# Turning the attention output by VectorE block transposes and a DRAM round trip instead of by TensorE, with key sums and row copies moved between engines

## The chip, the cores and the metric

The kernel runs on one core of one Trainium2 chip. The metric is the device time of one execution in microseconds (us), a median over repeated executions. Where a few per cent or less matter, both kernels were timed in rounds on the same chip.

## The reference

Hash attention over q, k, v of shape (4, 8, 768, 64) is followed by an MLP mixer with a token and a channel stage:

```python
q_bits = (np.einsum('bhsd,dk->bhsk', q, proj) > 0)          # 6 hash bits, k alike
mask = q_bucket[:, :, :, None] == k_bucket[:, :, None, :]
scores = np.where(mask, scale * np.matmul(q, k.transpose(0, 1, 3, 2)), -1000000000.0)
...                                                          # softmax over keys, times v
x = attn_out.transpose(0, 2, 1, 3).reshape(B, S, H * D)      # (4, 768, 512)
xt = x.transpose(0, 2, 1)
h = np.maximum(xt @ w_tok1, 0.0) @ w_tok2                    # token stage
u = x + h.transpose(0, 2, 1)
h2 = np.maximum(u @ w_ch1, 0.0) @ w_ch2                      # channel stage
return (u + h2).astype(np.float32)
```

## The kernel before

Attention runs over 16 pairs of heads, four pairs to a batch, and each pair in two halves of 384 queries. It leaves its output in `XT`, with channels on the partitions. The first token product sums over positions, so it needs positions on the partitions. `turn` makes that layout `x` from `XT` with TensorE transposes and ScalarE copies.

```python
def turn(b, x, bank):
    for r in range(0, NR, 2):
        ps = bank()
        for k in range(2):
            at = S * b + P * (r + k)
            for cb in range(NCB):
                nc.tensor.transpose(ps[:, k, P * cb : P * cb + P], XT[:, cb, at : at + P], ident)
        nc.scalar.copy(x[:, r : r + 2], ps)
```

`turn` for batch 0 stands near the end of attention. For batches 1 to 3 it stands in the token stage:

```python
def mix1(b):                                   # first token product
    x = (x0, x1)[b % 2]
    if b:
        turn(b, x, banks)
    ...                                        # 12 matmuls (24 rows of the trace), W1 against x, then Relu to r1
        job()                                  # one weight conversion for the channel stage
def mix2(b):                                   # second token product
    ...                                        # 16 matmuls (32 rows of the trace)
        nc.vector.tensor_tensor(u, ps[:, :HALF], u, op=ALU.add)      # u is a part of XT
        if cb % 2:
            job()
for b in range(B):
    mix1(b)
    if b:
        mix2(b - 1)
...
mix2(B - 1)
```

Weights come as 64-bit numbers. A conversion of 768 columns takes one ScalarE instruction and two on VectorE (`begin`), one more on VectorE with two on GpSimd (`join`), and a Square on ScalarE with a last VectorE instruction (`end`). During attention one third of a conversion is done in each half.

For each pair the exponentials are added up over the six key blocks of a half, partly on GpSimd:

```python
self.a = ...;  nc.gpsimd.tensor_tensor(self.a, es[0], es[1], op=ALU.add)
nc.vector.tensor_tensor(self.d, es[2], es[3], op=ALU.add)
nc.vector.tensor_tensor(self.d, self.d, es[4], op=ALU.add)
...                                            # then es[5], then self.a
```

TensorE sums these over the partitions (`sums`). VectorE refines the reciprocal, copies its rows to their neighbours (`nc.vector.tensor_copy(rec[other...], rec[at...])`), and multiplies (`divide`) into `XT`.

## Time and profile before

The kernel takes 862.65 us (median of 3, 862.43 to 862.66). TensorE's work divides the profiled execution (span 860.9 us) into stages. The first end is read from the chain that ended last, which has a start some 0.07 us later than the timeline's row.

| stage | ends with | at us | length |
|---|---|---|---|
| start | first scores of the first pair's second half | 16.86 | 16.86 |
| attention | first token product | 327.41 | 310.55 |
| token | first channel product | 423.20 | 95.79 |
| channel | VectorE's last addition | 856.9 | 433.7 |
| end | last store landed | 860.9 | 4.0 |

A row of a timeline gives the start, the length, the engine, the line of the program, the operation with its operands and shapes, and the number of instructions in the row. If the engine was idle before it, the length of that and what released it stand in brackets. A row of the view of waits gives the engine, its tile and line, what it waited for, and then the total, the number of times and the longest. The two kernels' line numbers differ. L567, L580 and L586 of before (first token product, second token product, VectorE's update of `XT`) are L598, L617 and L623 of the changed kernel.

Eight token products of about 10.35 us from start to start are 82.8 us of the token stage. The rest of its 95.79 us is transposes (10.4) and a wait of 2.5 us. A matmul of fp32 numbers is two rows of the trace, a transpose one; counts of matmuls below are counts of such rows.

### The profile page before, as it was taken

What the parts mean: (1) busy time and instruction counts of PE and PEld (TensorE: products, weight loads), DVE (VectorE), ACT (ScalarE), POOL (GpSimd) and SP (SyncE); (2) the same over time, 40 slices, a digit from 0 to 9 for tenths busy, and PEclk for the clock granted to TensorE, in tenths of its full rate; (3) what the DMA queues carried; (4) which work ended last, traced back from release to release, by engine and by line L of the source; (5) the groups of instructions that cost most, each with busy time, mean ns of one, the idle gap of its engine ahead of it and who ended that gap; (6) DMA issues with size and microseconds to landing.
All of it is one profiled execution on the core that took longest, in us unless ns stands there. A gap on an engine that the chain in (4) does not pass through costs nothing.

```text
span 860.9 us, 9280 instructions
## 1 busy us (share of the span) xinstructions
PE 847.9 (98%) x3545; PEld 395.2 (46%) x3545; DVE 558.2 (65%) x641; ACT 304.7 (35%) x445; POOL 214.2 (25%) x123
## 2 busy tenths in 40 slices
PE   8999999999999999998999999999999999999997
PEld 4444444444444454554544444444444444444444
DVE  3789999899899895899744483534457332336411
ACT  4666777667776673243012201012110101121000
POOL 3234244424524443166011111101101200011110
PEclk9999999999999999999999999999999999999999
DMA  4334232322332302132102201222210120000001
GB/s 150 106 115 155 112 113 77 112 113 76 115 130 89 130 28 79 68 111 72 38 0 74 73 0 62 86 98 73 73 37 18 43 97 12 1 0 1 24 25 53
DMA packets 20644, 61.16 MB, mean 71 GB/s; under 512 B 2800, under 2 KB 4464, under 8 KB 20592
## 3 DMA queue, kind: packets, MB, share of 16 engines
q1 hardware_dynamic: 20536, 60.46, 19.9%
q8 instruction: 30, 0.49, 0.2%
q14 instruction: 22, 0.18, 0.1%
q10 hardware_dynamic: 56, 0.02, 0.0%
HBM read 53.49 MB, written 6.29 MB: 69 GB/s over the span
## 4 chain that ended last, share of the span: by engine, by line
PE 91%; DVE 5%; DMA 1%; ACT 1%; issue 1%; SPq 0%; DVEq 0%; ACTq 0%
PE b L636 50%; PE sc L299 18%; PE acc L345 14%; PE t L580 3%; PE t L567 3%; PE hp L266 1%; PE sums L369 1%; DVE tmp L170 1%; DVE WC L196 1%; DVE tmp L167 1%; DMA raw<-in_moe_w_ch 1%; DMA qk<-in_qk 0%; DVE esd L334 0%; PE trp L226 0%; DVE T L537 0%
## 5 line engine op out<-in xcount | busy, mean ns | idle before, releaser
L306 ACT ACTIVATE e<-sc 128x768 f32<-128x768 f32 x192 | 151.6, 811 | 26.2 <-PE sc L299 25.6
L299 PE MATMUL sc<-qk 64*128 64x384 f32 x768 | 159.5, 495 | 0.7 <-ACT e L306 0.7
L643 ACT COPY p<-b 128x512 f32<-128x512 f32 x72 | 42.1, 585 | 304.6 <-PE b L636 304.6
L345 PE MATMUL acc<-e,vn 128*64 128x384 f32 x768 | 130.9, 490 | 0.0
L636 PE MATMUL b<-r,WC 128*128 128x512 f32 (+1 forms) x300 | 125.6, 575 | 0.0
L329 POOL TENSOR_TENSOR esa<-e 128x768 f32<-128x768 f32 x32 | 73.0, 2282 | 117.8 <-ACT e L306 101.9
L636 PE MATMUL b<-T,SW 128*128 128x512 f32 x216 | 96.6, 592 | 0.0
L299 PEld LDWEIGHTS sc<-qk 64*128 64x128 f32 x768 | 67.2, 188 | 56.9 <-issue 46.9
L636 PEld LDWEIGHTS b<-r,WC 128*128 128x128 f32 x300 | 57.0, 190 | 67.1 <-issue 64.1
L345 PEld LDWEIGHTS acc<-e,vn 128*64 128x64 f32 x768 | 52.3, 137 | 74.9 <-issue 73.0
L662 POOL TENSOR_TENSOR p<-p,p 128x512 f32<-128x512 f32 x18 | 22.7, 1262 | 249.4 <-ACT p L643 249.4
L185 POOL TENSOR_TENSOR tmp<-tmp,raw 128x768 f32<-128x768 f32 x20 | 43.7, 2183 | 124.8 <-DVE tmp L182 79.1
L666 DVE TENSOR_TENSOR r<-p,u 128x512 f32<-128x512 f32 x18 | 12.5, 693 | 91.4 <-ACT u L643 91.4
L636 PE MATMUL b<-T,WC 128*128 128x512 f32 x144 | 67.7, 592 | 0.0
L636 PEld LDWEIGHTS b<-T,SW 128*128 128x128 f32 x216 | 41.0, 190 | 51.7 <-issue 51.7
L636 PE MATMUL b<-XT,WC 128*128 128x512 f32 x144 | 64.7, 592 | 0.0
L299 PE MATMUL sc<-bits 64*128 64x384 bf16 x384 | 63.2, 323 | 0.7 <-DMA bits<-g 0.7
L636 PE MATMUL b<-r,SW 128*128 128x512 f32 x144 | 62.8, 592 | 0.0
L331 DVE TENSOR_TENSOR esd<-e 128x768 f32<-128x768 f32 x32 | 40.8, 1275 | 19.9 <-ACT e L306 19.9
L332 DVE TENSOR_TENSOR esd<-esd,e 128x768 f32<-128x768 f32 x32 | 45.1, 1408 | 3.3
L351 ACT ACTIVATE num<-acc,vsum 128x384 f32<-128x384 f32 x32 | 18.6, 580 | 80.3 <-PE acc L345 80.3
L186 POOL TENSOR_TENSOR tmp<-tmp 128x768 f32<-128x768 f32 x20 | 45.1, 2257 | 1.6
(84 smaller groups left out, 947.6 us busy)
## 6 DMA issues: line engine op xcount, KB each, us to landing
raw<-in_moe_w_ch SPq DMA_DIRECT2D x16, 768.0 KB
seen<-in_qk SPq DMA_DIRECT2D x16, 768.0 KB
qk<-in_qk SPq DMA_DIRECT2D x15, 768.0 KB
vn<-in_v SPq DMA_DIRECT2D x16, 384.0 KB
vt<-in_vT SPq DMA_DIRECT2D x16, 384.0 KB
out<-p SPq DMA_DIRECT2D x18, 256.0 KB
raw<-in_moe_w_tok SPq DMA_DIRECT2D x4, 768.0 KB
bits<-g SPq DMA_DIRECT2D x124, 5.2 KB
```

The lines of the kernel that those rows point to most:

```text
L185: nc.gpsimd.tensor_tensor(unit, unit, lo, op=ALU.mult)
L186: nc.gpsimd.tensor_tensor(big, big, unit, op=ALU.add)
L299: nc.tensor.matmul(sc[:, i, :HALF], t[rows, 1, P * c : P * c + P], t[rows, 0, qs], start=start, stop=not start,)
L306: nc.scalar.activation(e, sc[:, :, :HALF], ACT.Exp, scale=SCALE)
L329: nc.gpsimd.tensor_tensor(self.a, es[0], es[1], op=ALU.add)
L331: nc.vector.tensor_tensor(self.d, es[2], es[3], op=ALU.add)
L332: nc.vector.tensor_tensor(self.d, self.d, es[4], op=ALU.add)
L345: nc.tensor.matmul(acc[D * i : D * i + D], vn[:, i, c], e[:, i], start=(c == 0), stop=(c == NR - 1),)
L567: nc.tensor.matmul(ps, W1[:, r, P * j : P * j + P], x[:, r], start=(r == 0), stop=(r == NR - 1),)
L580: nc.tensor.matmul(ps[:, :HALF], r1[:, j, P * cb : P * cb + P], W2[:, j, HALF * half : HALF * half + HALF], start=(j == 0), stop=(j == NJ ...
L636: nc.tensor.matmul(self.ps[i][:, cols], left(k), right(k)[:, cols], start=first and k == ks[0], stop=k == ks[-1], skip_group_check=True,)
L643: nc.scalar.copy(c, self.ps[i])
```

## The change

The intent is to take the transposes off TensorE, the bound engine. VectorE turns 32x32 blocks, each where it stands. DMA writes the blocks of two pairs to DRAM in pieces of 256 B and reads a batch back in rows of 2 KB. To make room, GpSimd's additions and conversion steps go to VectorE without GpSimd beside them, ScalarE's first conversion step is folded into one of these, and ScalarE takes the reciprocal's row copies and the mask's product.

```diff
-    nc.sync.dma_start(out=projblk, in_=proj_pair)
+    nc.scalar.dma_start(out=projblk, in_=proj_pair)
 ...                                            # conversion
-            nc.gpsimd.tensor_tensor(unit, unit, lo, op=ALU.mult)
-            nc.gpsimd.tensor_tensor(big, big, unit, op=ALU.add)
+            nc.vector.scalar_tensor_tensor(unit, lo, 2.0**-52, unit, op0=ALU.mult, op1=ALU.mult)
+            nc.vector.tensor_tensor(big, big, unit, op=ALU.add)
 ...
+    def bounce(pool, n):
+        b, hp = pairs[n]
+        stage = pool.tile([P, S // 32, 2, 32], F32, name="stage", tag="stage", bufs=1)
+        for k in range(2):
+            nc.vector.transpose(
+                stage[:, :, k], XT[:, hp + k, S * b : S * b + S].rearrange("p (a i) -> p a i", i=32),
+            )
+        to = bounced[b].rearrange("(a i) (g c) -> g i a c", i=32, g=4)
+        for g in range(4):
+            nc.sync.dma_start(
+                out=to[g, :, :, 32 * hp : 32 * hp + 64],
+                in_=stage[32 * g : 32 * g + 32].rearrange("p a k i -> p a (k i)"),
+            )
+
+    def fetch(b, x):
+        nc.sync.dma_start(out=x, in_=bounced[b].rearrange("(r p) c -> p r c", p=P))
 ...                                            # mask, every pair but the first
+            if n:
+                nc.scalar.mul(g, g, bitscale)
 ...                                            # key sums: all on VectorE, no esa tile
-                        nc.vector.tensor_copy(rec[other : other + 32, h], rec[at : at + 32, h])
+                        nc.scalar.copy(rec[other : other + 32, h], rec[at : at + 32, h])
 ...                                            # attention: per two pairs, and after the last
+                if half and n and n % 2 == 0:
+                    bounce(pool, n - 2)
+                if half == 0 and n == 2 * NP:
+                    fetch(0, x0)
-        turn(0, x0, lambda: psum.tile([P, 2, 512], F32, name="trp", tag="sc", bufs=3))
         ...
         quotients.divide()
+        bounce(pool, len(pairs) - 2)
 ...                                            # token stage
+        if not turned:
+            fetch(1, x1)
         jobs = jobs(weights(pool)) if jobs else []
-            return psum.tile([P, 512], F32, name=name, tag="mm", bufs=4)
+            return psum.tile([P, 512], F32, name=name, tag="mm", bufs=4 if turned else 8)
+            if not turned and b + 2 < B:
+                fetch(b + 2, x)
```

Cut here are the reordering of `r1` that undoes the block order, one pair of weight sums that moves to the channel stage, and the last store, which is issued from ScalarE's queue.

More of the change, by code (lines that the diff above doesn't have):

```diff
@@ L160, in begin @@
             raw, to, rows = self.fetched.pop(0)
-            lo, hi = raw[:, :, 0], raw[:, :, 1]
+            hi = raw[:, :, 1]
             tmp = self.pool.tile([P, 2, NW], F32, name="tmp", tag="cvt", bufs=self.bufs - 1)
             big = tmp[:, 0].bitcast(U32)
-            nc.scalar.activation(lo.bitcast(F32), lo, ACT.Copy, scale=2.0**-52)
             nc.vector.tensor_scalar(
@@ L179, in join @@
             self.begun = None
-            lo, hi = raw[:, :, 0].bitcast(F32), raw[:, :, 1].bitcast(F32)
+            lo, hi = raw[:, :, 0], raw[:, :, 1].bitcast(F32)
             big, unit = tmp[:, 0], tmp[:, 1]
@@ L217 @@
     pairs = [(b, hp) for b in range(B) for hp in range(NP)]
+    dram = ctx.enter_context(tc.tile_pool(name="dram", bufs=1, space=bass.MemoryType.DRAM))
+    bounced = [dram.tile([S, DM], F32, name=f"bounced{b}") for b in range(B)]
+    def bounce(pool, n):
[13 more added lines that the diff above has]
+        nc.sync.dma_start(out=x, in_=bounced[b].rearrange("(r p) c -> p r c", p=P))
     def turn(b, x, bank):
@@ L273, in hashes @@
                 )
-                nc.vector.tensor_scalar(g[rows], g[rows], bitscale[rows], None, op0=ALU.mult)
+                if n == 0:
+                    nc.vector.tensor_scalar(g[rows], g[rows], bitscale[rows], None, op0=ALU.mult)
+            if n:
+                nc.scalar.mul(g, g, bitscale)
             for j in range(4):
@@ L327, in add @@
                 if k == 0:
-                    self.a = pool.tile([P, 2, HALF], F32, name="esa", tag="esa", bufs=2)
-                    nc.gpsimd.tensor_tensor(self.a, es[0], es[1], op=ALU.add)
                     self.d = pool.tile([P, 2, HALF], F32, name="esd", tag="esd", bufs=3)
-                    nc.vector.tensor_tensor(self.d, es[2], es[3], op=ALU.add)
-                    nc.vector.tensor_tensor(self.d, self.d, es[4], op=ALU.add)
-                else:
-                    nc.vector.tensor_tensor(self.d, self.d, es[5], op=ALU.add)
                     nc.vector.scalar_tensor_tensor(
-                        self.d, self.d, NR * EPS, self.a, op0=ALU.add, op1=ALU.add,
+                        self.d, es[0], NR * EPS, es[1], op0=ALU.add, op1=ALU.add,
                     )
+                for e in (es[2:4], es[4:])[k]:
+                    nc.vector.tensor_tensor(self.d, self.d, e, op=ALU.add)
             def weigh(self):
@@ L546, in tokens @@
         R1 = {}
+        turned = not jobs
+        if not turned:
+            fetch(1, x1)
         jobs = jobs(weights(pool)) if jobs else []
@@ L560, in mix1 @@
             x = (x0, x1)[b % 2]
-            if b:
+            if b and turned:
                 turn(b, x, banks)
@@ L569, in mix1 @@
                     )
-                nc.scalar.activation(r1[:, j], ps, ACT.Relu)
+                to = r1[:, j]
+                if not turned:
+                    to = to.rearrange("p (c g i) -> p g c i", c=NCB, i=32)
+                    ps = ps.rearrange("p (g c i) -> p g c i", c=NCB, i=32)
+                nc.scalar.activation(to, ps, ACT.Relu)
                 job()
             R1[b] = r1
+            if not turned and b + 2 < B:
+                fetch(b + 2, x)
         def mix2(b):
@@ L720, in outputs @@
                 for cols in parts:
+                    issuer = nc.scalar if final and cols.start else nc.sync
                     nc.vector.tensor_tensor(u[:, cols], x.ps[3][:, cols], u[:, cols], op=ALU.add)
                     at = slice(sl[0].start + cols.start, sl[0].start + cols.stop)
-                    nc.sync.dma_start(out=out[KC + m, :, at], in_=u[:, cols])
+                    issuer.dma_start(out=out[KC + m, :, at], in_=u[:, cols])
         unseen = list(range(len(pairs))) if judge else []
@@ L753, in channels @@
         inputs(0, T, 1)
+        sums = weight_sums(
+            WC2, SW2, slice(0, NHT // 2), slice(NHT // 2, NHT), slice(0, DM // 2), slice(DM // 2, DM),
+        ) if judge else []
         last = B * S // (2 * TT) - 1
@@ L760, in channels @@
                 rs.append(r)
+                if sums:
+                    sums.pop(0)()
                 if s or t:
@@ L809, in jobs @@
                 *[conversion.one] * n2,
-                *weight_sums(
-                    WC2, SW2, slice(0, NHT // 2), slice(NHT // 2, NHT),
-                    slice(0, DM // 2), slice(DM // 2, DM),
-                ),
             ]
```

## The prediction

> **What bounds the kernel now.** I read the page's busy shares first, then the chain that ended last, because a share is only an average over stages.
>
> ```profile
> PE 847.9 (98%) x3545; PEld 395.2 (46%) x3545; DVE 558.2 (65%) x641; ACT 304.7 (35%) x445; POOL 214.2 (25%) x123
> PE 91%; DVE 5%; DMA 1%; ACT 1%; issue 1%; SPq 0%; DVEq 0%; ACTq 0%
> ```
>
> TensorE is busy for 847.9 of 860.9 us, so only 13.0 us of the span are not matmul. Work taken from another engine pays only if TensorE waits for it; matmuls taken away pay in full unless a wait comes in their place. So I read TensorE's waits, and its timeline from the end of attention (attention ends at 327.4 us, the channel stage starts at 423.2):
>
> ```profile
> PE t L580 <- DVE XT L586: 2.5, 1, 2.5
> PE trp L226 <- ACT x L227: 1.9, 3, 1.4
> PE sums L369 <- DVE esd L335: 0.3, 1, 0.3
> ```
>
> ```profile
> 318.67 2.84 PE L226 MATMUL trp<-ident,XT 128*128 128x128 f32 x24
> 321.44 0.83 PE L369 MATMUL sums<-esd,ones 128*32 128x384 f32 x2
> ...
> 327.41 10.57 PE L567 MATMUL t<-x,W 128*128 128x512 f32 x24
> 337.81 1.91 PE L226 MATMUL trp<-ident,XT 128*128 128x128 f32 x16
> 341.14 1.09 PE L226 MATMUL trp<-ident,XT 128*128 128x128 f32 x8 [1.42 <-ACT x L227]
> 342.07 10.47 PE L567 MATMUL t<-x,W 128*128 128x512 f32 x24
> ```
>
> Here L226 is the transposition and L567 the first token product of one batch. A batch's transposition costs what lies between the starts around it: 321.44 - 318.67 = 2.77 us for batch 0, 342.07 - 337.81 = 4.26 us for batch 1, and 3.08 us each for batches 2 and 3 (the timeline has 362.69 to 365.77 and 386.39 to 389.47). Sum 13.19 us, with the 1.9 us wait for ScalarE's copies inside it.
>
> In attention VectorE is nearly full. One pair of heads, 19.6 us, in the table of stretches (columns: length, then PE, PEld, DVE, ACT, POOL busy time, clock, DMA share and GB/s):
>
> ```profile
> 247.50:267.10 19.60, 19.60 (x140) 9.06 (x136) 18.76 (x21) 13.25 (x20) 9.96 (x4) 1.00 0.24 83
> ```
>
> VectorE has 18.76 us of work in 19.60 but TensorE never waits. Much of VectorE's time is not its own; the same line costs two very different times:
>
> ```profile
> 301.46 0.96 DVE L335 SCALAR_TENSOR_TENSOR esd<-esd,esa 128x768 f32<-128x768 f32 x1
> 316.60 2.40 DVE L332 TENSOR_TENSOR esd<-esd,e 128x768 f32<-128x768 f32 x1
> 319.10 2.40 DVE L334 TENSOR_TENSOR esd<-esd,e 128x768 f32<-128x768 f32 x1
> ```
>
> All three are 128x768 operations with two inputs; the slow ones run while GpSimd does its own additions and products.
>
> **What the Trainium skill says.** (1) "SBUF — State Buffer", section "Who interferes with whom": a VectorE instruction with two SBUF inputs contends with a GpSimd instruction that reads SBUF, and the later one blocks. The trace agrees: 0.96 us alone, 2.40 beside GpSimd. (2) "VectorE: DVE Perf Modes", "The three transpose paths": VectorE transposes 32x32 blocks only, not 128x128. So the change needs DMA to put blocks in place; the kernel before has no such instruction, no run here shows its time yet. (3) "DMA: Bandwidth & Descriptors", "Specifications": under 512 B a transfer is not at line rate. The trace of before has no 256 B writes to DRAM. (4) "TensorE: Matmul & The Clock Gate", "Why this matters for your kernels": TensorE idle for over about 3 us drops back in rate. The trace agrees at the start: the first eight hash matmuls took 2.48 us in the chain, later eights 0.65 to 0.78.
>
> **The change, part by part.**
>
> *Transposes.* 96 TensorE transposes and 12 ScalarE copies go: -13.2 us on the path. In their place come 16 VectorE transposes of 128x768, one per pair; I take 0.95 us each, that of a 128x768 operation at one element per cycle (rows of 0.95 to 0.96). Per pair of the attention stage VectorE then does, uncontended: ten key-sum additions x 0.96 = 9.6; hash comparison 0.55; reciprocal 0.56 + 1.03 = 1.6; division 0.95; transpose 0.95; two thirds of a weight conversion of 0.56 + 0.96 + 0.56 + 3 x 0.96 = 5.0, thus 3.3. Sum 17.0 of 19.6 us. It removes 4 x 0.36 of row copies, one 0.58 mask product, and all blocking by GpSimd, which has nothing left to do in this stage. So VectorE fits, with less pressure than the 18.76 before, and gives nothing directly, as TensorE did not wait for it, except the 0.34 us wait for the last key sums, which should go.
>
> *ScalarE.* Per pair +4 row copies of about 0.41 us back to back (a 128x384 activation from SBUF takes 0.52 alone) and +1 mask product of 0.5, minus 0.6 (two thirds of a 0.92 us conversion step): 13.25 + 1.5 = 14.8 of 19.6 us. The danger is its order: the copies wait for VectorE's reciprocal and stand before the next exponentials. Walked by hand from the end of a pair's first scores (246.1): exponential of the sums ends at +2.7, reciprocal halves at +3.8 and +4.35, copies end at +5.7, the numerator at +6.3. The next exponentials started at +6.65 before. They still can; in one half of six a 0.92 us Square stands in between too, and even then the third score buffer is due at about +8.0, when the first exponential ends. Cost: 0 to 2 us in all.
>
> *Token stage.* PSUM banks for products go from 4 to 8 and GpSimd's conversion steps go to VectorE; its blocked instructions of about 2 us become 0.56 to 0.96. The 2.5 us wait of L580 should go. One pair of weight sums moves to the channel stage, where VectorE is busy for 190.6 of 437 us: hidden.
>
> *Ends.* The projection's load moves to ScalarE's queue, so the first query load is issued 0.4 us earlier (its predecessor's issue took 0.39): -0.4. The last store has a queue of its own: -0.3.
>
> *The new wait.* Batch 1 must come back from DRAM between two products. In the built order the SyncE queue has four writes of pair 15's block, then the read of batch 1, and the writes wait for the last division and its transposes. From the end of attention's last matmul (call it 0): numerator and division until 1.5 (before: 327.48 to 329.01), two transposes until 3.4, four issues of about 0.5 until 5.4, though data starts at about 4.9. Data: 4 x 768 pieces of 256 B, 192 per DMA engine. Packets of 2 KB took about 85 ns in the trace (146 packets in 8.7% of 16 x 8 us around 845 us); for 256 B I choose 35 to 45 ns, as the page on DMA leads me to expect poor rate: 7 to 9 us. Then 768 rows of 2 KB, 48 per engine, 4 us, and 0.7 for completion: batch 1 is there at about 17 to 18.5. The first product of batch 0 keeps TensorE busy until 10.3. So a **new wait of about 7 us**, plus about 1.5 for a cold TensorE after it (the cold eight at the start lost 2.48 - 0.78 = 1.7). Batches 2 and 3 have a whole product more of slack, and hide.
>
> Sum: 862.65 - 13.2 - 0.3 - 2.5 - 0.7 = 845.9; + 7 (wait) + 1.5 (cold) + 0.5 (ScalarE) = **855 us**: more than half of the gain is spent by one wait.
>
> **Rivals.** (a) *The trip is hidden*: small pieces flow at 20 ns or the read overtakes the writes. For it: DMA engines are busy for a quarter of the time only. Against: the writes stand before the read in one queue and depend on the last division. Even with no data time for the writes, the read is issued at 5.4 and lands near 11.5, after 10.3. Time 846 to 848. (b) *Small writes are far slower*, 60 to 100 ns each: wait of 12 to 20 us, time 859 to 867. In attention the 3072 small pieces per two pairs would then also hold up the mask rows behind them in the same queue, which land some 4 us before they are needed. (c) *ScalarE's order becomes the bound*: if copies take 0.6 us or VectorE runs late, each pair loses 0.5 to 1 us: +8 to +16 us, time 862 to 870. Against: 4.8 us of slack per pair, and the walk above. (d) *VectorE becomes the bound* if a transpose of 4-byte data takes twice as long: 18 of 19.6 us, still under, so little.
>
> **Range and chances.** The gains are sure to about 1 us, as they are TensorE time that is removed, 16.7 us in sum; with nothing lost the time would be 846, still 1.9% down, so faster by over 2% needs a gain that I don't see. Losses of 2 to 15 us give 848 to 861. Slower by over 2% needs a loss of 34 us.
>
> **What would show it.** Right: no TensorE transposes; TensorE busy near 835 us; VectorE's 128x768 additions all near 0.96 us in attention; one long TensorE wait in the token stage, before the first product of batch 1, put down to a DMA that reads the bounced tensor, 5 to 11 us; transposes near 0.95 us; no wait on L580's successor. Wrong: waits of score matmuls for exponentials once per pair (rival c), waits for the mask rows (b), or no wait before batch 1 (a). The prediction fails if small writes, the one cost that no row of before shows, are far from 40 ns, or if the order on ScalarE's queue bites.

## More of the kernel before

In the token stage whole conversions are the jobs. Their loads are issued on SyncE's queue.

## The result

The changed kernel takes **860.74 us** (median of 4, 859.76 to 861.67) against 862.65 us before (4 runs, 862.43 to 864.18). The ratio is 0.9974, with a 95% interval from 0.9956 to 0.9991. Ratios here are the mean time of one kernel's runs over that of the other's runs of the same rounds, so they are not quite the ratio of the medians quoted. A later timing of the same kernel (`e11_changed_again`) gave 860.24 us and 0.9964.

The time is inside the forecast range and inside 2%, as forecast. Of the forecast gain of 7.65 us, though, only some 2 us came (1.9 between these medians).

From the page of the changed kernel, its busy TensorE and its chain that ended last:

```profile
PE 842.5 (98%) x3449; PEld 386.3 (45%) x3449; DVE 530.8 (62%) x650; ACT 316.8 (37%) x492; POOL 52.8 (6%) x51
PE 88%; DVE 8%; DMA 2%; issue 1%; ACT 0%; SPq 0%; DVEq 0%; ACTq 0%
```

The 96 transposes are gone (3545 to 3449 matmuls), but TensorE's busy time fell by 5.4 us only. VectorE's share of the chain rose from 5% to 8% and DMA's from 1% to 2%. TensorE's longest waits in the changed kernel:

```profile
PE t L598 <- DMA x<-bounced: 3.8, 1, 3.8
PE t L617 <- DVE XT L623: 2.9, 1, 2.9
PE sc L324 <- DMA bits<-g: 1.3, 1, 1.3
```

The first is the forecast wait for batch 1 from DRAM. The second is the successor of L580's wait, which should have gone: it is still there and 0.4 us longer. The third, for the mask's rows at the start, was 0.7 us before.

TensorE's timeline of the changed kernel from the end of attention:

```profile
320.57 1.55 PE L390 MATMUL sums<-esd,ones 128*32 128x384 f32 x8
...
326.07 10.57 PE L598 MATMUL t<-x,W 128*128 128x512 f32 x24
340.46 13.61 PE L598 MATMUL t<-x,W 128*128 128x512 f32 x24 [3.82 <-DMA x<-bounced]
...
408.54 12.02 PE L617 MATMUL t<-W,r 128*128 128x384 f32 x32 [2.92 <-DVE XT L623]
420.39 3.60 PE L673 MATMUL b<-XT,WC 128*128 128x512 f32 x8
```

No transposes stand between products any more. But the product after each wait is also slow: 13.61 us where others of 24 take 10.46, and 12.02 where others of 32 take 10.48. The table of stretches of the changed kernel shows why (columns as in the prediction, the clock third from the end):

```profile
12.00:17.00 5.00, 4.36 (x22) 2.09 (x26) 2.88 (x3) 3.81 (x6) 0.00 (x0) 0.66 0.73 252
249.17:268.73 19.56, 19.56 (x138) 9.04 (x140) 17.30 (x21) 15.90 (x25) 0.00 (x0) 1.00 0.40 124
340.40:344.00 3.60, 3.54 (x4) 1.52 (x5) 1.43 (x2) 0.00 (x0) 0.00 (x0) 0.50 1.00 399
344.00:348.00 4.00, 4.00 (x8) 1.70 (x7) 3.86 (x6) 0.92 (x1) 0.00 (x0) 0.67 0.28 108
342.53:408.54 66.01, 63.09 (x167) 31.90 (x166) 64.41 (x83) 12.50 (x16) 0.00 (x0) 0.97 0.42 147
```

After the wait for batch 1 the granted clock is 0.50 until about 346.6, and slow matmuls count as busy. That is why TensorE's busy time fell so little. The first row shows the same at the start. The second row is one pair of heads in attention: TensorE full, VectorE 17.30 of 19.56 us, ScalarE 15.90, GpSimd nothing. The same table of the kernel before, around its start and its own 2.5 us wait:

```profile
12.00:17.00 5.00, 4.29 (x34) 1.89 (x35) 1.43 (x2) 4.43 (x6) 1.81 (x1) 1.00 0.68 205
405.10:407.60 2.50, 0.00 (x0) 0.00 (x0) 2.47 (x5) 0.91 (x1) 1.24 (x1) 1.00 0.00 0
407.60:412.00 4.40, 4.38 (x14) 2.66 (x15) 2.65 (x5) 0.00 (x0) 2.99 (x2) 1.00 0.00 0
```

There an idle time of 2.5 us left the clock at 1.00. Where the time went, stage by stage:

| stage | before | after | difference | forecast |
|---|---|---|---|---|
| start | 16.86 | 17.52 | +0.66 | -0.4 |
| attention | 310.55 | 308.55 | -2.00 | -2.77 - 0.34 + 0.5 = -2.6 |
| token | 95.79 | 94.32 | -1.47 | -10.4 - 2.5 + 7 + 1.5 = -4.4 |
| channel | 433.7 | 433.7 | 0 | 0 |
| end | 4.0 | 4.2 | +0.2 | -0.3 |
| span | 860.9 | 858.3 | -2.6 | -7.7 |

The token stage is the largest miss. What it waits for is seen in two other engines. SyncE's timeline of the changed kernel:

```profile
332.24 0.58 SPq L239 DMA_DIRECT2D x<-bounced  x1
332.87 19.12 SPq L154 DMA_DIRECT2D raw<-in_moe_w_ch  x4
```

VectorE's timeline of the changed kernel:

```profile
328.10 1.83 DVE L227 STREAM_TRANSPOSE stage<-XT 128x768 f32<-128x768 f32 x2
342.53 0.56 DVE L165 TENSOR_SCALAR tmp<-raw 128x768 uint32<-128x768 uint32 x1 [12.61 <-DMA raw<-in_moe_w_ch]
```

SyncE issues in program order. The four writes of the last two pairs wait for the last division and the two transposes, and are issued from 330.0 to 332.1. Only then, at 332.24, comes the read of batch 1. Its data had been in DRAM for long, and by then it waits for nothing but its place in the queue. (It could not have gone at any time: in e1 below, where it stands ahead of the writes, it still waits for the last scores to free its room in SBUF, and is issued at 316.38.) From 332.87 come the loads of the weights, of which the first lands at 342.53. VectorE has nothing to do for 12.61 us although all conversions of this stage are still ahead of it. From 342.53 to 408.54 it is busy for 64.41 of 66.01 us (the last row of the table of stretches above), and at the end of that it still keeps TensorE waiting. The chain that ended last goes this way: the writes' issue, the read's issue, the weights' load, VectorE's conversions, and then the products from 408.54.

The Trainium skill states what lies behind it in "DMA: Bandwidth & Descriptors", section "Anatomy of one DMA — SWDGE (gpsimd) path": the DMA engines don't wait on semaphores, the issuing sequencer does so before it dispatches. The trace agrees: everything behind the waiting writes was issued after 332.1, although it did not depend on them.

### The profile page after: what moved, and what is told of

The parts are those of the page before. It is cut to its first block, busy times and chain, and to the rows that moved or that the text cites. A ratio compares the mean times of both kernels' runs of the same rounds, so it can differ in the third digit from the quotient of the medians.

```text
span 858.3 us, 9068 instructions
## 1 busy us (share of the span) xinstructions
PE 842.5 (98%) x3449; PEld 386.3 (45%) x3449; DVE 530.8 (62%) x650; ACT 316.8 (37%) x492; POOL 52.8 (6%) x51
## 4 chain that ended last, share of the span: by engine, by line
PE 88%; DVE 8%; DMA 2%; issue 1%; ACT 0%; SPq 0%; DVEq 0%; ACTq 0%
PE b L673 50%; PE sc L324 19%; PE acc L366 15%; PE sums L390 2%; PE t L617 1%; PE hp L288 1%; DVE tmp L184 1%; DVE tmp L168 1%; DMA raw<-in_moe_w_ch 1%; DVE XT L623 1%; DVE WC L195 1%; DVE tmp L180 1%; DVE tmp L165 1%; DVE tmp L185 1%; DMA qk<-in_qk 1%
## 5 line engine op out<-in xcount | busy, mean ns | idle before, releaser
L358 DVE TENSOR_TENSOR esd<-esd,e 128x768 f32<-128x768 f32 x128 | 122.3, 955 | 10.0
L598 PE MATMUL t<-x,W 128*128 128x512 f32 x96 | 45.1, 629 | 3.8 <-DMA x<-bounced 3.8
L617 PE MATMUL t<-W,r 128*128 128x384 f32 x128 | 43.5, 499 | 2.9 <-DVE XT L623 2.9
L354 DVE SCALAR_TENSOR_TENSOR esd<-e 128x768 f32<-128x768 f32 x32 | 30.6, 956 | 21.8 <-ACT e L331 21.6
L680 ACT COPY u<-b 128x512 f32<-128x512 f32 x24 | 14.1, 587 | 79.1 <-PE b L673 79.1
L673 PEld LDWEIGHTS b<-T,WC 128*128 128x128 f32 x144 | 27.4, 190 | 34.4 <-issue 34.4
```

The source lines that it names most:

```text
L354: nc.vector.scalar_tensor_tensor(self.d, es[0], NR * EPS, es[1], op0=ALU.add, op1=ALU.add,)
L358: nc.vector.tensor_tensor(self.d, self.d, e, op=ALU.add)
L598: nc.tensor.matmul(ps, W1[:, r, P * j : P * j + P], x[:, r], start=(r == 0), stop=(r == NR - 1),)
L617: nc.tensor.matmul(ps[:, :HALF], r1[:, j, P * cb : P * cb + P], W2[:, j, HALF * half : HALF * half + HALF], start=(j == 0), stop=(j == NJ ...
L673: nc.tensor.matmul(self.ps[i][:, cols], left(k), right(k)[:, cols], start=first and k == ks[0], stop=k == ks[-1], skip_group_check=True,)
L680: nc.scalar.copy(c, self.ps[i])
```

## Experiments

Theory Q (the queue's order; the expectations call it theory A, and count their rivals from B): the weights' loads and the read of batch 1, both held behind the last writes, are two separate limits of the token stage. Rivals: the wait for batch 1 alone is the loss; the clock after the waits is the loss; the trip through DRAM is dear in itself; ScalarE's copies are the loss; or the changes of engines gain nothing and only the trip does. The first four kernels ran with the kernel before at 863.64 us (7 runs, 862.64 to 865.97). All kernels gave a correct result. The runs were on three chips (e1 to e4, e5 to e8, e9 to e11), so kernels of different groups are compared by their ratios to the kernel before.

### e1_read_first: the read of batch 1 ahead of the last writes

```diff
         quotients.divide()
-        bounce(pool, len(pairs) - 2)
 ...
             fetch(1, x1)
+            bounce(pool, len(pairs) - 2)
         jobs = jobs(weights(pool)) if jobs else []
```

> Only the read of batch 1 is moved ahead of the last pair's four writes; the weight loads stay behind the writes. Theory A (two losses side by side: TensorE waits for batch 1, and VectorE starts its conversions 12.6 us late because the weight loads stand behind writes and read; the later one sets the end): the wait before batch 1's product goes (3.8 us and the half clock after it, 3.1), but the wait for VectorE in the last products grows, since conversions start only some 4 us earlier than in the changed kernel. Time about 856, that is 4 to 5 us below the changed kernel. Rival B (the wait for batch 1 is the whole loss on the path): 6.9 us below, about 853.8, and no longer wait for VectorE.

Measured: 858.52 us (857.25 to 859.17), ratio 0.9935 (0.9912 to 0.9957). TensorE's timeline, then VectorE's:

```profile
325.81 20.87 PE L598 MATMUL t<-x,W 128*128 128x512 f32 x48
405.20 13.64 PE L617 MATMUL t<-W,r 128*128 128x384 f32 x32 [4.88 <-DVE XT L623]
```

```profile
339.19 0.56 DVE L165 TENSOR_SCALAR tmp<-raw 128x768 uint32<-128x768 uint32 x1 [9.53 <-DMA raw<-in_moe_w_ch]
```

The wait for batch 1 is gone (48 matmuls without a gap), and most of it comes back as a longer wait for VectorE with a slow product after it, behind two short waits for VectorE of 0.26 and 1.28 us. The time is above the 856 that the theory gave, which had left these out. The token stage is 92.87 us, from 94.32. From VectorE's first conversion to the release of the last products it is 405.20 - 339.19 = 66.0 us; in the changed kernel it was 408.54 - 342.53 = 66.0 us. So the wait for batch 1 lay beside VectorE's path and was not the loss by itself.

### e2_weights_first: the weights' loads ahead of the last writes, the read behind them

```diff
         turned = not jobs
+        jobs = jobs(weights(pool)) if jobs else []
         if not turned:
+            bounce(pool, len(pairs) - 2)
             fetch(1, x1)
-        jobs = jobs(weights(pool)) if jobs else []
```

(The call at the end of attention is removed as in e1.)

> The first two weight loads are moved ahead of the last pair's writes; the read of batch 1 stays behind them. Theory A: VectorE starts at about 331 instead of 342.5, the 2.9 us wait for VectorE and the 1.6 us of half clock after it go, the wait for batch 1 (3.8 us) and its half clock (3.1 us) stay; about 856, 4 to 5 us below. Rival B: nothing gained, 860 to 861, as only the wait for batch 1 counts.

Measured: 857.32 us (857.23 to 858.05), ratio 0.9926 (0.9905 to 0.9946). TensorE's timeline:

```profile
342.11 12.95 PE L598 MATMUL t<-x,W 128*128 128x512 f32 x24 [5.72 <-DMA x<-bounced]
...
407.40 10.59 PE L617 MATMUL t<-W,r 128*128 128x384 f32 x32 [0.79 <-DVE XT L623]
```

Now VectorE starts converting at 329.59 and its wait shrinks to 0.79 us. The read comes later still, and the wait for batch 1 grows to 5.72 us. The stage is 92.01 us.

### e3_both_first: one weight load, the read, the second load, then the last writes

```diff
-            for _ in range(bufs - 1 or 1):
+            for _ in range(first or bufs - 1 or 1):
                 self.fetch()
 ...
+        conversion = weights(pool, 2) if jobs else None
         if not turned:
             fetch(1, x1)
+            conversion.fetch()
+            bounce(pool, len(pairs) - 2)
+        jobs = jobs(conversion) if jobs else []
```

> First weight load, read of batch 1, second weight load, and only then the last pair's writes. Theory A: both waits and both spells of half clock go, 3.8 + 3.1 + 2.9 + 1.6 = 11.4 us below the changed kernel, about 849; the first token product to the channel stage takes about 83 us instead of 94.3. If the writes themselves slow the other transfers (rival C, DMA bandwidth and not order), 2 to 5 us of wait for batch 1 remain and the time is 852 to 856.

Measured: **849.50 us** (849.10 to 849.67), ratio 0.9831 (0.9811 to 0.9852). TensorE's timeline, then VectorE's:

```profile
325.95 20.87 PE L600 MATMUL t<-x,W 128*128 128x512 f32 x48
399.17 10.59 PE L619 MATMUL t<-W,r 128*128 128x384 f32 x32 [0.80 <-DVE XT L625]
```

```profile
329.72 0.52 DVE L165 TENSOR_SCALAR tmp<-raw 128x768 uint32<-128x768 uint32 x1
```

The stage is 83.65 us, against the 82.8 of its eight products. The same instructions run, only the issue order differs from the changed kernel: SyncE issues the first load at 302.62, the read at 316.52, the second load at 326.06, and the writes from 329.8 on. Freeing the read alone gained 1.45 us of the stage, freeing the loads alone 2.31, and both together 10.67. Theory Q is shown: two limits lie side by side, and with either gone the other holds the end. The trip through DRAM, with its 256 B pieces, can be hidden whole.

### e4_warm: dummy matmuls on TensorE while batch 1 is awaited

```diff
             R1[b] = r1
+            if not turned and b == 0:
+                ps = bank("warm")
+                for _ in range(9):
+                    nc.tensor.matmul(ps, W1[:, 0, :P], x[:, 0], start=True, stop=True)
```

> Changed kernel with nine idle matmuls (about 3.9 us) between the first two token products, so that TensorE does not sit idle while it waits for batch 1. The granted clock should stay at 1.00 there, and batch 1's product take 10.5 us instead of 13.6. Theory A: TensorE then reaches the last products 3.1 us earlier and waits for VectorE longer by as much: 860 to 861, no gain. Rival D (the clock drop is on the path by itself): 3.1 us below, about 857.6.

Measured: 858.81 us (856.75 to 860.97), ratio 0.9948 (0.9919 to 0.9978). TensorE's timeline:

```profile
335.22 7.89 PE L611 MATMUL warm<-x,W 128*128 128x512 f32 x18
342.94 10.46 PE L598 MATMUL t<-x,W 128*128 128x512 f32 x24
...
406.71 10.59 PE L621 MATMUL t<-W,r 128*128 128x384 f32 x32 [1.74 <-DVE XT L627]
```

I had mis-sized the filler: each fp32 matmul is two rows of the trace, so nine took 7.89 us and ran past the arrival of batch 1. The time of this run therefore settles little; its executions also fall in two groups (856.75 and 857.20 at a mean clock of 0.999, 860.41 and 860.97 at 0.995). The trace is clear on two things. With TensorE kept busy the next product takes 10.46 us instead of 13.61. And the last products are still released 66.0 us after VectorE's first conversion (340.71 to 406.71), and VectorE is busy for 64.40 us of these, with the same 83 instructions. The half clock after the wait for batch 1 was real, but it too lay beside VectorE's path. The profiled execution, one of the faster two, is still 3.3 us shorter than the changed kernel's, near the rival's 3.1, but for other reasons: 1.26 us by a start without a clock drop, 0.56 in what comes before VectorE's first conversion, and 1.43 because the last products ran at full clock after a wait of only 1.74 us. So the half clock behind the wait for VectorE does lie on the path.

### e5 to e7: three details on top of e3

These ran with e8 and the kernel before at 863.71 us (9 runs, 862.19 to 866.09). e5 puts the row copies back on VectorE, e6 puts the projection's load back on SyncE's queue, and e7 adds five small dummy matmuls ahead of the first mask products.

```diff
# e5_rows_on_vector
-                        nc.scalar.copy(rec[other : other + 32, h], rec[at : at + 32, h])
+                        nc.vector.tensor_copy(rec[other : other + 32, h], rec[at : at + 32, h])
# e6_proj_on_sync
-    nc.scalar.dma_start(out=projblk, in_=proj_pair)
+    nc.sync.dma_start(out=projblk, in_=proj_pair)
# e7_start_fill
                         if c == GR - 1:
+                            for _ in range(5):
+                                nc.tensor.matmul(idle[:D, :D], ones, ones, start=True, stop=True)
```

> On top of the better order: the reciprocal's row copies go back from ScalarE to VectorE. Theory: in every sixth half a Square stands behind the copies on ScalarE and scores take 5.28 us instead of 5.05; five such halves, 1.2 us. With the copies on VectorE all halves take 5.05, and the time falls by about 1 us, if VectorE (82 per cent busy in attention) has room for 1.4 us more per pair. If VectorE's room is short, its key sums come late and the gain is gone or turned into a loss of a few us.

e5 measured: 849.79 us (849.32 to 850.59), ratio 0.9842 (0.9828 to 0.9855). In the changed kernel and e3, five halves of scores take 5.26 to 5.29 us instead of 5.05. ScalarE's timeline of the changed kernel shows the order behind it:

```profile
290.69 2.08 ACT L411 COPY rec<-rec 32x384 f32<-32x384 f32 x4 [0.71 <-DVE rec L405]
292.78 0.91 ACT L194 ACTIVATE raw<-raw 128x768 f32<-128x768 f32 x1
293.59 0.56 ACT L372 ACTIVATE num<-acc,vsum 128x384 f32<-128x384 f32 x1
294.06 4.39 ACT L331 ACTIVATE e<-sc 128x768 f32<-128x768 f32 x6
```

The copies wait for the reciprocal, a conversion's Square follows, and the next half's exponentials come behind both. In e5 all halves take 5.05 us, so the copies are shown to cause the 1.2 us. But e5 won no time, because a wait for VectorE took its place. From TensorE's waits in e5:

```profile
PE sums L390 <- DVE esd L358: 1.6, 1, 1.6
```

> On top of the better order: the projection's load goes back to SyncE's queue, ahead of the query loads. Theory: the earlier start of the changed kernel leaves TensorE idle longer before the first mask rows (1.33 us instead of 0.72), the granted clock falls to about half from 12 to 15 us, and the second half's scores start at 17.5 instead of 16.9. With the load back, the clock stays at 1.00 and the second scores start near 16.9: about 0.7 us faster than without. Rival: the drop has nothing to do with it and stays, time the same or 0.4 slower.

e6 measured: 848.76 us (848.23 to 850.44), ratio 0.9834 (0.9820 to 0.9848).

> On top of the better order: five idle matmuls of 64x64 stand before the first mask products, where TensorE waits 1.3 us for the mask rows. Theory (idle time draws the clock down): clock 1.00 from 12 to 16 us, second scores start at about 16.1, 1.4 us faster. Rival (the drop comes of something else, such as the cold start itself): clock still near 0.5 from 12 to 15 us, nothing gained.

e7 measured: 848.26 us (847.92 to 849.07), ratio 0.9824 (0.9811 to 0.9837). In both profiles the clock stays at 1.00 from 12 to 17 us. The first pair's second-half scores start at 16.54 (e6) and 16.26 (e7) instead of e3's 17.45, and the wait for the mask rows is 0.67 and 0.60 us. So the start's loss of about 1 us is a matter of the clock. The times don't show the forecast 0.7 and 1.4 us: the intervals of the ratios of e3, e6 and e7 overlap.

Whether the edits did it is not shown. The packed traces record the steps of the clock. In all 13 profiles every spell between two steps is a whole multiple of 3.413 us (only the last is cut by the end; before the first step the record is silent, and views print 1.00), so the steps lie on a grid, and the grid lies elsewhere in each execution. Where a point of the grid falls between 11.3 and 12.8 us (the changed kernel, e1, e2, e3, e5, e8, e9, e10, e11), the clock fell at that point; where none does (before, e4, e6, e7), it did not. (This split was found afterwards. The first eight hash matmuls split the profiles the same way: busy for under 2.0 us in the nine, 2.3 or more in the four. The first recorded step up is at 4.5 to 5.9 us in the nine and at 6.7 to 10.0 in the four.) The projection's load is on SyncE in e9 as in e6, and e10 has e7's filler, yet both fell; e4 has neither and did not. The executions' mean clocks point to some effect of the edits: 0.999 or more in four of five for e6 and for e7 and in none of the nine of e3 and e5, but also in two of four for e4, e8 and e10. What drops the clock at the start stays open.

### e8_engines_only: the moves between engines, with TensorE's transposes kept

`turn` is called as in the kernel before, there is no DRAM trip, and everything else is as in the changed kernel.

```diff
-                if half and n and n % 2 == 0:
-                    bounce(pool, n - 2)
 ...
+        turn(0, x0, lambda: psum.tile([P, 2, 512], F32, name="trp", tag="sc", bufs=3))
 ...
-        bounce(pool, len(pairs) - 2)
 ...
-        turned = not jobs
+        turned = True
```

> Only the moves between engines (key sums and conversions on VectorE, row copies and mask product on ScalarE, loads' queues, later weight sums), with TensorE's transposes kept and no trip through DRAM. Theory: TensorE did not wait for VectorE in attention, so nothing is gained there and 1.2 us lost by ScalarE's order; VectorE's conversions without GpSimd run ahead in the token stage, so the 2.5 us wait of the last products goes or shrinks. Time 1 to 3 us below the kernel before. If GpSimd's blocking was what held the kernel, it would be 5 us or more below.

Measured: 862.19 us (860.97 to 863.66), ratio 0.9979 (0.9964 to 0.9995). The wait of the second token product for VectorE is 1.3 us instead of 2.5, and the waits of the transposes are 1.1 instead of 1.9. The slow start (second-half scores at 18.84) and five halves of 5.28 us stand against it. The moves alone are worth next to nothing (0.2%).

### e9_trip_only: the trip in e3's order, with the work left on the engines of before

Key sums, conversions, row copies, the mask and the projection's load are as in the kernel before; the trip is issued as in e3. To fit in SBUF, the buffers of GpSimd's partial sum went from two to one, which may add to the result.

```diff
-                    nc.vector.scalar_tensor_tensor(
-                        self.d, es[0], NR * EPS, es[1], op0=ALU.add, op1=ALU.add,
-                    )
+                    self.a = pool.tile([P, 2, HALF], F32, name="esa", tag="esa", bufs=1)
+                    nc.gpsimd.tensor_tensor(self.a, es[0], es[1], op=ALU.add)
 ...
-                        nc.scalar.copy(rec[other : other + 32, h], rec[at : at + 32, h])
+                        nc.vector.tensor_copy(rec[other : other + 32, h], rec[at : at + 32, h])
```

> Only the trip through DRAM, in the better order of transfers; key sums, conversions, row copies and mask product stay where they were before, with GpSimd beside VectorE (GpSimd's sum has one buffer instead of two, for the transposes' staging tile needs the room). Theory: VectorE, which had 18.76 us of work in 19.6 per pair, gets 0.95 more and runs late; key sums come late for TensorE, at the end of attention and perhaps in every pair: attention 3 to 15 us longer, which eats part of the 13 us of transposes removed. Time 851 to 862. If VectorE's blocked time gives way instead, about 849, as with the whole change in the better order.

Measured: 867.34 us (866.39 to 867.88) with the kernel before at 864.02 us on the same chip (7 runs, 862.37 to 866.17), ratio 1.0038 (1.0014 to 1.0061), above the 851 to 862 expected. TensorE's timeline in e9:

```profile
331.36 1.50 PE L392 MATMUL sums<-esd,ones 128*32 128x384 f32 x6 [5.13 <-DVE esd L358]
```

VectorE falls behind over attention, and at its end TensorE waits 5.1 us for the last key sums, with a slow product after it (5.54 us for 24 matmuls that took 4.09 before). Later, TensorE waits 3.3 us for VectorE in the token stage. The additions beside GpSimd take 2.4 to 2.6 us, against 0.955 us in the changed kernel. So neither half of the change pays alone, beyond the 0.2% of e8. The moves make VectorE's room, and the trip uses it.

### e10_combined and e11_changed_again

e10 is e3 with e7's filler and with the row copies on VectorE in all but the last two pairs, where e5's wait had come from. e11 is the changed kernel unedited, for a second timing on e9's and e10's chip.

```diff
-                        nc.scalar.copy(rec[other : other + 32, h], rec[at : at + 32, h])
+                        copy = nc.vector.tensor_copy if self.n < len(pairs) - 2 else nc.scalar.copy
+                        copy(rec[other : other + 32, h], rec[at : at + 32, h])
```

> The better order of transfers, five idle matmuls at the start, and row copies on VectorE except in the last two pairs. Expected: 849.5 minus 1.2 (clock at the start) minus 1.2 (five halves back to 5.05 us) with no wait for late sums beyond the 0.7 us before: about 847. If the gains hide behind each other, 848 to 849.

e10 measured: **847.32 us** (846.29 to 848.11), ratio 0.9806 (0.9782 to 0.9830), the lowest median of all, though not clear of e7 by its interval, and unclear as to 2%. All halves but one (5.14, where the copies are on ScalarE) take 5.04 to 5.05 us, and the wait of e5 is gone. Its profile had the slow start despite the filler.

> The changed kernel itself, unedited, on the chip of these runs, so that it and the combined one stand against the same runs of before: ratio to before 0.9974 again, within 0.002; if this chip gives another ratio, the comparisons between chips above are worth less.

e11 measured: 860.24 us (859.73 to 861.58), ratio 0.9964 (0.9941 to 0.9988). The waits are 3.6 us for batch 1 and 4.1 us for VectorE. From VectorE's first conversion (341.9) to the release of the last products (407.95) it is 66.0 us again. The products behind the two waits take 12.26 and 12.28 us here, where the first profile had 13.61 and 12.02.

## Why the prediction was right or wrong

**What bounds the kernel, and the transposes.** Right. The 96 TensorE transposes went, batch 0's 2.77 us with them. With the order mended (e3) their removal in the token stage pays in full: the stage is within 0.9 us of its eight products.

**VectorE in attention.** Right: 17.30 us per pair for a forecast 17.0, the additions at a mean of 0.955 and 0.956 us, and the 16 transposes at a median of 0.955 us for the chosen 0.95.

The last key sums took 1.48 us from start to start instead of 1.95, so the forecast 0.34 us came (0.47).

**ScalarE.** Right in its mechanism, a little small in its terms. A row copy measured 0.511 us for the forecast 0.41 and a mask product 0.60 for 0.5, so a pair has 15.90 us of work for 14.8. The order on ScalarE cost 1.2 us in five halves, inside the 0 to 2 us that the walk gave but above the 0.5 in the sum.

**"The 2.5 us wait of L580 should go."** This is the step that failed. The reasoning looked at the length of VectorE's instructions, and these did shorten as said. It did not ask when VectorE's input arrives. The prediction listed SyncE's order for batch 1 ("four writes of pair 15's block, then the read of batch 1") but stopped there. The weights' loads were next in the same queue, and VectorE stood idle for 12.61 us. Afterwards the 66.0 us that it took up to the release of the last products set the end of the stage: 16.46 us until the first conversion, 66.0, and 11.85 for the last products, together the 94.3 us measured. In place of going, the wait grew by 0.4 us, with 1.5 us more for the slow product behind it: +1.9 for the forecast -2.5.

**The new wait for batch 1.** Right in its place and its cause, and too large: 3.8 us, for 7 in the sum and "5 to 11" as its sign in the profile. The mis-sized term is the small pieces. The 3072 of the last writes flowed from 330.8 to 334.4, so 192 per DMA engine in 3.6 us, or 19 ns each for the 35 to 45 chosen. The read behind them took 5.9 us (334.4 to 340.3) for the forecast 4, as it shared the engines with the weights' loads. Batch 1 was there at 14.3 us after attention's last matmul instead of 17 to 18.5. (The division shown for the 85 ns of a 2 KB packet gives 76; leaving out the 18 small packets, at most 87.) More important, the sum treated this wait as lying on the path that sets the end. e1 and e4 show that it lay beside VectorE's path. TensorE's waits in one stage were added up as if independent, where the later of two paths counts.

**"About 1.5 for a cold TensorE."** Too small in this profile. The product after the wait for batch 1 lost 3.1 us (13.61 against 10.46), and the later one 1.5 us (12.02 against 10.48). In e11, the same kernel, both lost 1.8 us, behind waits of 3.60 and 4.05. The half clock lasted two periods of the 3.413 us grid in the first case (339.8 to 346.6) and one in the other three, so the cost is not set by the wait's length alone. I had sized it from eight matmuls at the start. These agree less with the page on the clock than the prediction says: they ran before the clock's first recorded step up (10.0 us), but behind an idle time of 1.03 us only.

The errors partly cancelled. Waits and slow products of the token stage were forecast at -2.5 + 7 + 1.5 = +6.0 us against before and came to +1.94 + 3.82 + 3.15 = +8.9, so the stage gained 1.5 us instead of 4.4.

**The ends.** Wrong, both small. The start was to gain 0.4 us and lost 0.66, at a granted clock of 0.66 in the stretch from 12 to 17 us; the cause of the drop stays open. The last store's own queue gave nothing (4.2 us for 4.0).

**TensorE's busy time** was forecast near 835 us and was 842.5, since matmuls at half clock count as busy.

**The rivals.** (a) had the speed of the small pieces (19 ns for its 20), but with this order of issue the trip was not hidden for that; e3 shows that it is hidden by the order. (b) did not come, and (c) only as the 1.2 us above. (d) had the right engine for the wrong reason: VectorE did become the path that ends last, through late input and not through slow transposes. None of the four named the weights' loads.

## What to carry to other kernels

When a transfer is added to a queue whose issuer works in order, list everything that stands behind it there, and issue first what depends on nothing. Do not add up the waits of the bound engine in one stage: lay out each path (here the read, and VectorE with its loads) and take the later, because freeing one alone gains little (1.5 and 2.3 us here, 10.7 together). When an idle time of a few microseconds is forecast, count the slow matmuls after it as well.

## What the Trainium skill lacked or had wrong

- "TensorE: Matmul & The Clock Gate", sections "Why this matters for your kernels" and "What's actually happening": the first warns of gaps over about 3 us, the second says that the window of about 3.4 us runs freely. As a fixed limit the first is not what the runs show. In the changed kernel the clock halved at 408.04, when TensorE had been idle for 2.42 us of a gap of 2.92; a gap of 2.52 us in the kernel before left it at 1.00. The free-running window fits: all steps lie on a grid of 3.413 us. Eight gaps of 2.9 to 5.7 us cost 1.5 to 3.2 us of matmul time each, not in order of their length (3.1 behind 3.82, 1.8 behind 3.60, 2.5 behind 5.72).
- The same page has no numbers on a drop soon after the start without such a gap. In 9 of 13 profiles the clock fell between 11.3 and 12.8 us, around waits of 0.6 to 1.3 us between small matmuls, for one or two periods of the grid, at a cost of about 1 to 2 us.
- "VectorE: DVE Perf Modes", section "The three transpose paths", has a time for one 128x128 bf16 tile only, and no page has a measured time for fp32. 128x768 fp32 elements in 32x32 blocks took 0.955 us, the same as an addition of that shape.
- "DMA: Bandwidth & Descriptors", section "Specifications", says that transfers under 512 B miss line rate, without a rate (the page has an overhead for 256 B further down). For writes to DRAM the runs show 19 ns per 256 B piece and engine over the whole flow, some 218 GB/s over 16 engines (786 KB in 3.6 us), and 283 GB/s at its fastest (333 to 334 us), where 2 KB rows and weights flowed at 397 GB/s right after (337 to 340 us).
